# Attention and a top-1 mixture of experts on one core: six experts sorted by their token counts, with three capacities in place of one

## The chip, the cores and the metric

The kernel runs on one core of a Trainium2 chip. The metric is the device time of one execution in microseconds (us); three runs of the kernel before gave 747.33, 748.36 and 748.40 us, with a median of 748.36 us.

## The reference

Eight batches of eight heads attend causally over 576 positions with a multiplicative decay; the result, 4608 rows of 512 numbers, goes through a layer of eight experts of which each row takes one.

```
scores = q @ k.T / sqrt(64) + decay          # causal, decay from the cumulated log of f
x      = softmax(scores) @ v                 # 4608 rows x 512
logits = x @ w_gate                          # 512 x 8
e(row) = argmax(logits);  g(row) = softmax(logits)[e]
out[row] = g(row) * relu(x[row] @ w1[e]) @ w2[e]     # w1: 512 x 1024, w2: 1024 x 512
```

All inputs are float32. On the inputs that the reference draws, experts 0 to 7 receive 582, 620, 632, 571, 592, 462, 604 and 545 rows, 4608 in all.

## The kernel before

**Attention.** The first 297 us compute attention and store its rows in device memory (`x_dram`). The order of all its steps is a table of words in `attention_all` (lines 639 to 697): a word names a step, and an object that pins the program order keeps each engine to that order. After each batch, routing (`route_stages`) ranks the batch's rows within their experts; after the last batch `table_indices` (line 1049) turns the table of ranks into three arrays of 40 columns: the row to gather (`gi_fast`), the row to scatter to (`si_fast`), the gate weight (`g_fast`). Column 5e + m belongs to tile m, 128 rows, of expert e. In the table of words this is `34.ix`; `34.ef3` and `34.ef4` gather the last two tiles of expert 0, `34.en` two tiles of expert 1, `34.et3` and `34.et4` transpose the two tiles of expert 0 on TensorE.

**Experts.** Every expert has room for `CAP` = 640 rows, five tiles of 128. A slot beyond an expert's count gathers row 0, and its result is scattered to a row number out of bounds, which the scatter leaves out. Expert 0 is interleaved with the end of attention; experts 1 to 7 run one after another in `Moe.run`, each in two phases.

- *Up* (`seven`, `product`): the 640 rows are split in two halves of 320, the weight matrix in four blocks, and Strassen's method in Winograd's form makes the product out of seven block products. There are four rounds `i` of seven products, and a product is six matmuls of 128 x 128 weights on 320 columns (line 1456: two halves of the contraction, and for each float32 product three rounded products). That makes 4 x 7 x 6 = 168 matmuls for each expert. ScalarE, VectorE and GpSimd sum, apply relu and split the result into a high and a low word.
- *Down* (`down`, line 1244): for each tile of 128 rows 24 matmuls, with the rows of the hidden layer as stationary weights and 512 columns of `w2` streaming. Between them stand the transposes of the next expert's gathered rows (`turn_t`, line 1412, four for each tile). The last tile of the last expert is done in two halves of 256 columns (`down_last`, line 1267).

Weights of the next expert are loaded on SyncE's queue (SP) by `load_s` (line 1334, four DMAs of 128 KB, four times for each expert) and `load_v` (line 1380, four DMAs of 512 KB); GpSimd forms the sums of weight blocks from them (`sums_s`, lines 1340 to 1343), ScalarE and VectorE split them in two words. All steps are placed by a step number (`ups`, `dns`) and issued in that order.

**Overflow.** After the last expert `overflow` (line 1608) computes on VectorE how many rows exceed the room, loads that number into a register of every engine (line 1635), and repeats a loop (line 1639) once for each 128 rows left over. With all counts up to 640 the loop is passed over.

Of the kernel before, what the change touches and what calls it, by code (L numbers as in the profile page):

```python
# [10 lines left out]
I32 = mybir.dt.int32  # L11
# [30 lines left out]
XM = 2 * (KT // 2) * HN  # L42
XN = ("T2", "T1", "T4", "T3", "B22")
# [142 lines left out]
def attention_all(c, tc, qkT, va, vb, f, wgd, x_dram, batch_done, more_consts, extra):  # L186
# [11 lines left out]
    with ExitStack() as st:  # L198
# [413 lines left out]
        def fin_logits(b, part, pool):  # L612
# [82 lines left out]
            34.W07 34.d21 34.d02 34.d12 34.ix 34.ef3 34.d22 34.ef4 34.en 34.d13 34.et3:m 34.et4:c  # L695
# [397 lines left out]
class Moe:  # L1093
    def __init__(self, c, tc, x_dram, w1, w2, out):
        self.c, self.tc, self.nc = c, tc, tc.nc
        self.x_dram, self.w1, self.w2, self.out = x_dram, w1, w2, out
        self.w1p, self.w2p, self.xg, self.x, self.h = {}, {}, {}, {}, {}
        self.idx, self.w1raw, self.w2raw, self.py = {}, {}, {}, {}

        self.ups = 5  # L1100
# [88 lines left out]
    def index(self, e, m):  # L1189
        if e == 0 and m < NA:  # L1190
            return (*self.idx["early"], m)
        return (*self.idx["all"], e * NST + m)

# [31 lines left out]
    def rows_of_h(self, e, m):  # L1225

        if e == 0:
            h = self.h[0, 0 if m < NA else 1]
            ms = slice((m % NA) * P, (m % NA) * P + P)
            return lambda i, ft: h[i][:, ft, ms]  # L1230
        return lambda i, ft: self.h[e][i][:, ft, m * P : m * P + P]

    def down(self, e, m, part=(0, FT), pool=None):

        c, nc = self.c, self.nc
        rows = self.rows_of_h(e, m)
        _, si, g, s = self.index(e, m)
        if part[0] == 0:
            self.py[m] = psum(pool or (c.ps_v, c.ps_m)[m % 2])
        py = self.py[m]  # L1240
        for ft in range(*part):
            w = self.w2p[e, ft]
            for k, (hi_, wi) in enumerate(((0, 0), (0, 1), (1, 0))):
# [7 lines left out]
        nc.scalar.activation(y, py, AF.Copy, scale=g[:, s : s + 1])  # L1251
        self.scatter(y, si[:, s : s + 1])
# [38 lines left out]
    def steps(self):  # L1291
# [17 lines left out]
        def indices():  # L1309
# [8 lines left out]
            en=lambda: (self.fetch(1, 3), self.fetch(1, 4)),  # L1318
# [58 lines left out]
    def load_v(self, e, i):  # L1377
# [4 lines left out]
            self.w2[e, 2 * i * P : 2 * i * P + 2 * P, :].rearrange("(f p) d -> p f d", p=P),  # L1382
# [10 lines left out]
    def begin_t(self, e):  # L1393

        c = self.c
        xa = c.xap.tile([P, 2, KT, HN], F32R, name="xa", tag="xa")
        part = lambda a: a.rearrange("p (k s) -> p k s", s=HN)
# [6 lines left out]
    def turn_t(self, e, m):  # L1404
# [34 lines left out]
        z = min(max(HN - m * P, 0), P)  # L1439
        if z < P:  # L1440
            second(pt[:, :, z:], m * P + z - HN)
# [3 lines left out]
    def split_t(self, e, n, eng=None):  # L1445

        c, k = self.c, XN.index(n)
        self.round(c.words["X", k, 0], c.words["X", k, 1], c.values["X", k, 1], eng)

    def product(self, e, i, bank, part, mat, x, start):  # L1450
# [3 lines left out]
        for kt in range(KT // 2):  # L1454
            for wi, xi in ((0, 0), (1, 0), (0, 1)):
                self.nc.tensor.matmul(  # L1456
                    bank[:, 0:HN], w[:, wi, mat, kt], x[xi][:, kt, :],
# [4 lines left out]
    def seven(self, e, i, run, tasks):  # L1462
# [5 lines left out]
        a, b, g, d = (t[:, 0:HN] for t in (a, b, g, d))  # L1468
        p1, p5, u2, u3 = (self.up_.tile([P, HN], F32, name=f"u{k}") for k in range(4))
        hh, hl = self.h[e]  # L1470

        def place(h, f, n):
            return h[:, f * (FT // 2) + i, n * HN : n * HN + HN]
# [41 lines left out]
    def run(self, run, rest):  # L1515
        c, tc = self.c, self.tc
        T = lambda f, *args: lambda: f(*args)
        fetch = lambda e, m: T(self.fetch, e, m)
# [37 lines left out]
        with tc.tile_pool(name="moe_h", bufs=1) as hp, tc.tile_pool(name="moe_u", bufs=1) as up_, \  # L1556
# [3 lines left out]
            h = [t.rearrange("p (f s) -> p f s", s=CAP) for t in (c.words["hh"], hl)]  # L1560
            G = self.nc.gpsimd
            for e in range(1, E):
                self.h[e] = h
# [18 lines left out]
                if e + 1 < E:  # L1582
# [4 lines left out]
                    at(dns, (0, N(self.begin_t)), (0, N(self.turn_t, 3)), (0, fetch(e + 1, 1)),  # L1587
                       (0, N(self.split_s, 0, 0)), (1, N(self.split_s, 0, 1)),
                       (2, N(self.load_s, 2)), (2, N(self.turn_t, 4)),
                       (3, N(self.split_s, 1, 0)), (4, N(self.turn_t, 2)),  # L1590
                       (5, N(self.split_s, 1, 1)), (6, N(self.load_s, 3)),
                       (6, N(self.turn_t, 0)), (7, N(self.sums_s, 2)),
                       (8, N(self.turn_t, 1)), (9, N(self.split_s, 2, 0)),
# [9 lines left out]
                downs(e, range(NST - (e == E - 1)), dns)  # L1603
                if e == E - 1:
                    run(lambda: self.down_last(e, NST - 1))


def overflow(c, tc, x_dram, w1, w2, out):
# [5 lines left out]
    with ExitStack() as st:  # L1614
# [4 lines left out]
        V.tensor_scalar(ex, c.carry, -float(CAP), 0.0, ALU.add, ALU.max)  # L1619
# [19 lines left out]
        with tc.For_i(0, n_it) as _i:  # L1639
# [13 lines left out]
            V.tensor_scalar(rr, rr, float(P), float(CAP) - 8192.0 * E, ALU.mult, ALU.add)  # L1653
# [144 lines left out]
```

## Time and profile before

| | before |
|---|---|
| median of three runs | 748.36 us (747.33 to 748.40) |
| the profiled execution | 747.16 us |
| its span, first to last instruction | 744.9 us |
| granted TensorE clock, mean | 0.998 |
| TensorE matmul busy | 736.4 us, 99% |
| VectorE busy | 552.3 us, 74% |
| ScalarE busy | 486.1 us, 65% |
| GpSimd busy | 430.6 us, 58% |

The profiled execution took 2.3 us more than its span, and lies 1.2 us under the median of the three runs. Busy shares are means over the whole program; a stage can have another limit than the program.

### The profile page before, as it was taken

The page shows a single profiled execution, that of the slowest core. Times are in us where ns is not written, and L with a number is a line of the kernel's source. Part 1 is how long each engine was busy: PE and PEld are TensorE (multiplying, and loading weights), DVE is VectorE, ACT ScalarE, POOL GpSimd, SP SyncE. Part 2 cuts the span into 40 slices and gives each one's busy share as a digit, 9 for nine tenths or more (in the row PEclk, how much of TensorE's full clock was granted, in tenths as well). Part 3 has the DMA queues.
Part 4 walks back from the last instruction along what each step waited for, and adds up shares of the span by engine and source line. Part 5 has one row for each costly group of instructions (what it writes and reads, how often), then busy time and mean ns, then how long its engine had stood idle before and what let it go on. Part 6 is the DMA issues. An engine that isn't in the chain of part 4 may idle for free.

```text
span 744.9 us, 16310 instructions
## 1 busy us (share of the span) xinstructions
PE 736.4 (99%) x5552; PEld 612.6 (82%) x5552; DVE 552.3 (74%) x1553; ACT 486.1 (65%) x1267; POOL 430.6 (58%) x594
## 2 busy tenths in 40 slices
PE   9999999999999999999999999999999999999996
PEld 6667777777777777989998998998998988988985
DVE  8877989888889998555888488487586685784720
ACT  7899899898989996335566465464564653663621
POOL 6643656566565586634976575475475565566311
PEclk9999999999999999999999999999999999999999
DMA  7989898898989694534453523613623632523100
GB/s 221 238 211 218 217 236 224 227 233 222 243 206 248 179 258 144 174 114 127 123 170 113 181 73 114 201 57 109 205 73 100 201 97 92 180 86 126 54 29 34
DMA packets 82932, 118.41 MB, mean 159 GB/s; under 512 B 9823, under 2 KB 40543, under 8 KB 82848
## 3 DMA queue, kind: packets, MB, share of 16 engines
q1 hardware_dynamic: 75680, 97.18, 47.8%
q0 software_dynamic: 6400, 19.93, 8.1%
q8 instruction: 45, 0.74, 0.4%
q14 instruction: 39, 0.32, 0.1%
q10 hardware_dynamic: 768, 0.25, 0.1%
HBM read 98.14 MB, written 20.22 MB: 159 GB/s over the span
## 4 chain that ended last, share of the span: by engine, by line
PE 94%; POOL 2%; DVE 1%; issue 1%; DMA 0%; ACT 0%; SPq 0%; POOLq 0%; ACTq 0%
PE ps L1244 28%; PE ps L1456 19%; PE ps L548 12%; PE ps L488 12%; PE ps L418 10%; PE ps L1214 4%; PE ps L454 2%; PE pr L1456 1%; PE ps L1412 1%; PE ps L605 1%; PE ps L1267 1%; PE pr L270 1%; PE pr L1037 1%; DVE w_1w L1371 0%; POOL w1r L1341 0%
## 5 line engine op out<-in xcount | busy, mean ns | idle before, releaser
L405 ACT ACTIVATE sc<-sc,nmx 128x128 f32<-128x128 f32 (+3 forms) x256 | 142.8, 566 | 3.0 <-DVE nmx L402 2.7
L1456 PE MATMUL ps<-X_0w,w1s 128*128 128x320 f32 x504 | 112.0, 309 | 0.0
L1244 PE MATMUL ps<-w_0w,hhw 128*128 128x512 f32 x272 | 108.7, 400 | 0.0
L1244 PE MATMUL ps<-w_1w,hhw 128*128 128x512 f32 x272 | 106.9, 393 | 0.0
L1244 PE MATMUL ps<-w_0w,hl 128*128 128x512 f32 x272 | 106.3, 391 | 0.0
L402 DVE CUSTOM_DVE_ANT_0 sc<-ps,dec 128x384 f32<-128x384 f32 (+2 forms) x192 | 90.2, 507 | 10.7 <-ACT sc L405 2.2
L1276 POOL DMA_INDIRECT out<-y,si_fast x37 | 37.5, 1012 | 94.6 <-ACT y L1251 81.8
L548 PE MATMUL ps<-aT,va_t 128*64 128x256 f32 (+3 forms) x896 | 92.1, 353 | 0.0
L1456 PEld LDWEIGHTS ps<-X_0w,w1s 128*128 128x128 f32 x504 | 84.2, 188 | 0.2
L548 PEld LDWEIGHTS ps<-aT,va_t 128*64 128x64 f32 x896 | 57.4, 137 | 31.9 <-issue 6.4
L418 PE MATMUL ps<-raw 64*128 64x256 f32 (+3 forms) x512 | 81.6, 444 | 0.6 <-ACT aT L484 0.4
L1456 PE MATMUL ps<-X_1w,w1s 128*128 128x320 f32 x252 | 77.9, 309 | 0.0
L1251 ACT ACTIVATE y<-ps,g_fast 128x512 f32<-128x512 f32 x36 | 24.8, 690 | 80.7 <-PE ps L1244 59.2
L484 ACT COPY aT<-ps 128x512 f32<-128x512 f32 (+4 forms) x154 | 63.0, 452 | 12.2 <-PE ps L488 10.9
L418 PEld LDWEIGHTS ps<-raw 64*128 64x128 f32 x512 | 45.5, 186 | 26.1 <-issue 7.9
L1244 PEld LDWEIGHTS ps<-w_0w,hl 128*128 128x128 f32 x272 | 51.1, 188 | 11.3
L1498 POOL TENSOR_TENSOR u<-u,u 128x320 f32<-128x320 f32 x28 | 24.6, 880 | 61.4 <-DVE u L1496 61.3
L1244 PEld LDWEIGHTS ps<-w_0w,hhw 128*128 128x128 f32 x272 | 51.0, 188 | 10.1
L1361 DVE TENSOR_TENSOR w1s<-w1r,w1s 128x1024 fp32r<-128x1024 f32 (+1 forms) x42 | 53.2, 1279 | 8.3 <-ACT w1s L1355 8.3
L1456 PE MATMUL ps<-xa,w1s 128*128 128x320 f32 x336 | 58.7, 310 | 0.4 <-ACT u L1485 0.4
L1244 PEld LDWEIGHTS ps<-w_1w,hhw 128*128 128x128 f32 x272 | 51.1, 188 | 9.4
L1355 ACT CAST w1s<-w1r 128x1024 fp32r<-128x1024 f32 (+1 forms) x56 | 52.2, 944 | 8.7 <-POOL w1r L1341 8.0
(283 smaller groups left out, 1792.5 us busy)
## 6 DMA issues: line engine op xcount, KB each, us to landing
dec<-cd SPq DMA_DIRECT2D x30, 512.0 KB, 6.2
w1r<-in_w SPq DMA_DIRECT2D x112, 128.0 KB, 3.3
w<-in_w SPq DMA_DIRECT2D x28, 512.0 KB, 4.8
raw<-in_qkT SPq DMA_DIRECT2D x63, 160.0 KB, 6.1
raw<-in_qkT SPq DMA_DIRECT2D x64, 144.0 KB, 6.1
decj<-cd SPq DMA_DIRECT2D x30, 288.0 KB, 5.3
va_t<-in_va SPq DMA_DIRECT2D x32, 256.0 KB, 6.2
x_dram<-row SPq DMA_DIRECT2D x32, 256.0 KB, 5.5
```

The costliest lines, as they stand in the source:

```text
L402: V.tensor_tensor_reduce(dst, src, m, -0.125, init, ALU.add, ALU.min, out)
L405: nc.scalar.activation(x, x, AF.Exp, bias=nmx, scale=-1.0, accum_out=acc)
L418: note(nc.tensor.matmul(banks[j][:, o : o + w], r[:, P * t : P * t + P], r[:, QW : QW + w], start=True, stop=n > 1))
L484: nc.scalar.copy(dst, src)
L488: note(nc.tensor.transpose(out.bitcast(F32R), words, c.identr))
L548: c.last_av = note(nc.tensor.matmul(pv[j * HD : (j + 1) * HD, q0 - qa : qb - qa], l, r, start=(blk == 0), stop=(blk == nb - 1),))
L1214: c.note(nc.tensor.matmul(ph[:, 0:n], w[:, wi, fs], x[xi][:, kt, :], start=(k == 0), stop=(k == 3 * KT - 1),))
L1244: c.note(nc.tensor.matmul(py, rows(hi_, ft), w[wi], start=(ft + k == 0), stop=(ft == FT - 1 and k == 2),))
L1276: self.nc.gpsimd.indirect_dma_start(out=self.out, out_offset=bass.IndirectOffsetOnAxis(ap=rows, axis=0), in_=y, in_offset=None, bounds_che ...
L1355: self.nc.scalar.copy(t[:, 0], raw)
L1361: (eng or self.nc.vector).tensor_tensor(lo, raw, hi.bitcast(F32), ALU.subtract)
L1456: self.nc.tensor.matmul(bank[:, 0:HN], w[:, wi, mat, kt], x[xi][:, kt, :], start=start and k == 0, stop=k == 5, skip_group_check=True,)
```

## The change

The experts 0 and 1 keep room for 640 rows. The experts 2 to 7 are sorted on the chip by their counts, largest first, and take the six places 2 to 7 of the program in that order, with room for 640, 640, 640, 576, 576 and 512 rows (`CAPS`). With 576 rows the halves have 288 columns, with 512 they have 256; a place of 576 has a last tile of 64 rows, the place of 512 has four tiles.

`sort` (`34.so`, seven VectorE operations) makes a key from each count, compares all pairs, and gives the expert's number for each place as an integer; `sort_table` (`34.st`, ten operations) puts the three index arrays into the order of the places by a masked sum. `expert` loads the expert's number from SBUF into a register of SP, once for each place, and `load_s` and `load_v` use that register in the addresses of the weights. `overflow` compares each count with its own capacity.

The diff, cut:

```diff
+NF = 2
+SORTED = E - NF
+CAPS = [CAP] * (E - 3) + [576, 576, 512]
...
-            34.W07 34.d21 34.d02 34.d12 34.ix 34.ef3 34.d22 34.ef4 34.en 34.d13 34.et3:m 34.et4:c
+            34.W07 34.d21 34.so 34.d02 34.d12 34.ix 34.ef3 34.d22 34.ef4 34.en 34.st 34.d13 34.et3:m 34.et4:c
...
+        if e >= NF:
+            return (*self.idx["sorted"], (e - NF) * NST + m)
...
+    def sort(self):
...
+        V.scalar_tensor_tensor(keys, c.carry[:, NF:E], float(E), c.iota128[:, NF:E],
+                               ALU.mult, ALU.add)
...
+        V.tensor_tensor(sel, keys.unsqueeze(1).to_broadcast([P, n, n]),
+                        keys.unsqueeze(2).to_broadcast([P, n, n]), ALU.is_gt)
...
+        V.tensor_reduce(rank, sel, AX.X, ALU.add)
...
+        V.tensor_copy(c.ids, ids)
...
+    def sort_table(self):
...
+        for nm, x in (("gi", gi), ("si", si), ("g", g)):
...
+            t = rp.tile([P, n, NST, n], F32, name="so_w")
...
+            V.tensor_reduce(y.rearrange("p (s m) -> p s m", m=NST), t, AX.X, ALU.add)
...
+    def expert(self, e):
...
+            v = self.nc.values_load(self.c.ids[0:1, e - NF : e - NF + 1],
+                                    engines=[mybir.EngineType.SP], min_val=NF, max_val=E - 1)
...
-        py = self.py[m]
+        n = min(P, CAPS[e] - m * P)
+        py = self.py[m][0:n]
...
+        w = self.expert(e)
         block = lambda f, d: self.w1[
-            e, d * 2 * P : d * 2 * P + 2 * P, (f * (FT // 2) + i) * P :][:, 0:P].rearrange(
+            w, d * 2 * P : d * 2 * P + 2 * P, (f * (FT // 2) + i) * P :][:, 0:P].rearrange(
...
-            self.w2[e, 2 * i * P : 2 * i * P + 2 * P, :].rearrange("(f p) d -> p f d", p=P),
+            self.w2[self.expert(e), 2 * i * P : 2 * i * P + 2 * P, :].rearrange(
...
+        n = CAPS[e] // 2
+        a, b, g, d = (t[:, 0:n] for t in (a, b, g, d))
...
-        fetch = lambda e, m: T(self.fetch, e, m)
+        fetch = lambda e, m: T(lambda: m * P < CAPS[e] and self.fetch(e, m))
+        turn_t = lambda e, m: T(lambda: m * P < CAPS[e] and self.turn_t(e, m))
...
+                tiles = -(-CAPS[e] // P)
+                downs(e, range(tiles - (e == E - 1)), dns)
...
-        V.tensor_scalar(ex, c.carry, -float(CAP), 0.0, ALU.add, ALU.max)
+        caps = op.tile([P, E], F32, name="ov_caps")
+        V.memset(caps, float(CAP))
...
+        for s in range(SORTED):
+            V.tensor_scalar(capm[:, :, s], c.so_sel[:, s], float(CAPS[NF + s]), None, ALU.mult)
+        V.tensor_reduce(caps[:, NF:], capm, AX.X, ALU.add)
+        V.tensor_tensor(ex, c.carry, caps, ALU.subtract)
+        V.tensor_scalar(ex, ex, 0.0, None, ALU.max)
```

Three places of the program show how instructions move.

VectorE at the end of routing, before; `tab` is the table of ranks, `xb` the low word of expert 0's last two tiles:

```order
L1041 TENSOR_TENSOR tab<-tab,pr 128x240
L1055 SCALAR_TENSOR_TENSOR ti_fast<-tab 128x40
L1057 CAST gi_fast<-ti_fast 128x40
L1059 TENSOR_SCALAR tu_fast<-tab 128x40
L1060 TENSOR_TENSOR ti_fast<-ti_fast,tu_fast 128x40
L1062 CAST si_fast<-ti_fast 128x40
L1064 TENSOR_TENSOR g_fast<-tab 128x40
L1065 TENSOR_TENSOR g_fast<-g_fast,tab 128x40
L1185 TENSOR_TENSOR xb<-ps,xb 128x4x128 x2
```

The same place with the change, as far as the index that the gathers wait for:

```order
L1044 TENSOR_TENSOR tab<-tab,pr 128x240
L1205 SCALAR_TENSOR_TENSOR so_key<-rk,iota_336 128x6
L1208 TENSOR_TENSOR so_sel<-so_key 128x36
L1211 TENSOR_REDUCE so_rank<-so_sel 128x6
L1213 TENSOR_TENSOR so_sel<-so_rank,iota_336 128x36
L1217 TENSOR_TENSOR so_t<-so_sel,iota_336 128x36
L1219 TENSOR_REDUCE so_ids<-so_t 128x6
L1221 CAST so_idi<-so_ids 128x6
L1058 SCALAR_TENSOR_TENSOR ti_fast<-tab 128x40
L1060 CAST gi_fast<-ti_fast 128x40
L1062 TENSOR_SCALAR tu_fast<-tab 128x40
```

The seven operations of `sort` stand between the table and `gi_fast`, `tu_fast`; the ten of `sort_table` follow `g_fast` and stand before `xb`.

SP, where the loads of expert 1's `w2` end and those for place 2 begin, before:

```order
L1334 DMA w1r<-in_w 128x2x128 x4
L1380 DMA w_0_1_94<-in_w 128x2x512 x2
L1380 DMA w_1_1_100<-in_w 128x2x512 x2
L1334 DMA w1r<-in_w 128x2x128 x16
L1380 DMA w_0_1_94<-in_w 128x2x512 x2
```

and with the change:

```order
L1447 DMA w_0_1_94<-in_w 128x2x512 x2
L1447 DMA w_1_1_100<-in_w 128x2x512 x2
L1254 TENSOR_LOAD so_idi
L1254 ISA x2
L1401 ISA
L1401 DMA w1r<-in_w 128x2x128
```

A load of a register with two instructions behind it comes once for each place, and from there on each DMA has an instruction of its own ahead of it.

VectorE at the end of the program, before:

```order
L1619 TENSOR_SCALAR ov_ex<-rk 128x8
L1626 MEMSET ov_one 128x8
L1634 MEMSET ov_cnt 128x1
L1622 TENSOR_TENSOR ov_cm<-ov_ex,iotaP 128x288
L1624 TENSOR_REDUCE ov_ex<-ov_cm 128x8
L1628 SCALAR_TENSOR_TENSOR ov_inc<-ov_one,ov_ex 128x8
L1630 TENSOR_TENSOR ov_exc<-ov_inc,ov_ex 128x8
L1632 CAST ov_tot<-ov_inc 1x1
```

and with the change:

```order
L1695 MEMSET ov_caps 128x8
L1698 TENSOR_SCALAR ov_capm<-so_sel 128x6 x6
L1708 MEMSET ov_one 128x8
L1716 MEMSET ov_cnt 128x1
L1699 TENSOR_REDUCE ov_caps<-ov_capm 128x6
L1700 TENSOR_TENSOR ov_ex<-rk,ov_caps 128x8
L1701 TENSOR_SCALAR ov_ex<-ov_ex 128x8
L1704 TENSOR_TENSOR ov_cm<-ov_ex,iotaP 128x288
L1706 TENSOR_REDUCE ov_ex<-ov_cm 128x8
L1710 SCALAR_TENSOR_TENSOR ov_inc<-ov_one,ov_ex 128x8
L1712 TENSOR_TENSOR ov_exc<-ov_inc,ov_ex 128x8
L1714 CAST ov_tot<-ov_inc 1x1
```

Nine operations more stand ahead of the integer that every engine loads.

## Rows read from the trace of the kernel before

**Rows 1.** The page: the span and its instructions
```profile
span 744.9 us, 16310 instructions
```

**Rows 2.** Stretches: length, then busy PE, PEld, DVE, ACT, POOL, clock, DMA share
```profile
632.66:657.30 24.64, 24.64 (x170) 24.64 (x169) 18.39 (x32) 15.23 (x29) 14.64 (x13) 1.00 0.47 144
686.68:711.31 24.63, 24.63 (x169) 24.63 (x169) 18.35 (x33) 15.23 (x29) 7.26 (x6) 1.00 0.21 77
```

**Rows 3.** Chain that ended last, experts 6 and 7: start, us, what
```profile
642.34 11.44 PE ps L1456 x78
...
711.31 21.97 PE ps L1244 x96
733.28 5.45 PE ps L1267 x48
```

**Rows 4.** The same chain while expert 0 ends
```profile
332.60 0.64 PE ps L1179 x8
...
336.09 5.75 PE ps L1214 x48
```

**Rows 5.** Groups by line and form, and the chain: matmuls with 64-column weights
```profile
L548 PE MATMUL ps<-aT,va_t 128*64 128x256 f32 x384 | 47.8, 384 | 0.0
...
L548 PE MATMUL ps<-aT,va_t 128*64 128x192 f32 x256 | 31.7, 326 | 0.0
...
L548 PE MATMUL ps<-aT,va_t 128*64 128x320 f32 x128 | 23.5, 445 | 0.0
...
L548 PE MATMUL ps<-aT,vb 68*64 68x64 f32 x128 | 9.1, 220 | 0.0
L548 PE MATMUL ps<-aT,va_t 128*64 128x64 f32 x128 | 9.1, 220 | 0.0
...
127.58 2.87 PE ps L548 x32
```

**Rows 6.** Timeline of VectorE and GpSimd at the end of routing, and the gathers' landing
```profile
326.12 0.20 DVE L1055 SCALAR_TENSOR_TENSOR ti_fast<-tab 128x40 f32<-128x40 f32 x1
326.36 0.18 DVE L1057 CAST gi_fast<-ti_fast 128x40 uint32<-128x40 f32 x1
326.45 0.18 DVE L1059 TENSOR_SCALAR tu_fast<-tab 128x40 f32<-128x40 f32 x1
...
326.82 1.09 POOL L1165 DMA_INDIRECT xg<-x_dram,gi_fast  x1 [2.89 <-DVE tu_fast L1059]
328.21 0.95 POOL L1165 DMA_INDIRECT xg<-x_dram,gi_fast  x1 [0.30 <-issue]
...
DMA to landing us min/median/max: 3.4/3.4/3.4
```

**Rows 7.** Lines L1635 and L1334 on SP: ns min/median/max
```profile
L1635 SPq TENSOR_LOAD <-ov_tot x1: 469/469/469, 740.5 to 740.5; - x1
...
L1635 SPq FUSED_REGOPS  x1: 186/186/186, 741.0 to 741.0; - x1
...
L1334 SPq DMA_DIRECT2D w1r<-in_w x112: 367/465/1121, 320.9 to 669.7; - x112
```

**Rows 8.** Expert 7's weight loads: SP, landing, and the sums on GpSimd
```profile
663.38 6.84 SPq L1334 DMA_DIRECT2D w1r<-in_w  x8
...
DMA to landing us min/median/max: 2.1/2.7/3.6
...
671.83 0.77 POOL L1340 TENSOR_TENSOR w1r<-w1r 128x256 f32<-128x256 f32 x1
...
677.77 1.34 POOL L1340 TENSOR_TENSOR w1r<-w1r 128x256 f32<-128x256 f32 x1
```

**Rows 9.** The end: VectorE, the last scatter, and what SP waited for
```profile
738.76 0.17 DVE L1619 TENSOR_SCALAR ov_ex<-rk 128x8 f32<-128x8 f32 x1 [25.09 <-PE ps L1267]
...
739.51 0.98 POOL L1276 DMA_INDIRECT out<-y,si_fast  x1 [4.19 <-ACT y L1271]
740.24 0.13 DVE L1632 CAST ov_tot<-ov_inc 1x1 int32<-1x1 f32 x1
...
SPq L1639 <- DMA out<-y,si_fast: 0.6, 1, 0.6
```

**Rows 10.** DMA queues, whole span: the gathers and scatters (packets, MB, share)
```profile
q0 software_dynamic: 6400, 19.93, 8.1%
```

More of the change, by code (lines that the diff above doesn't have):

```diff
@@ new lines, in sort_table @@
+    def sort_table(self):
+        c, nc = self.c, self.nc
+        V, rp, n = nc.vector, c.rp, SORTED
+        gi, si, g = self.idx["all"]
+        mine = []
+        for nm, x in (("gi", gi), ("si", si), ("g", g)):
+            if nm != "g":
+                x_ = rp.tile([P, n * NST], F32, name=f"so_{nm}f")
+                V.tensor_copy(x_, x[:, NF * NST :])
+            else:
+                x_ = x[:, NF * NST :]
+            t = rp.tile([P, n, NST, n], F32, name="so_w")
+            V.tensor_tensor(
+                t, c.so_sel.unsqueeze(2).to_broadcast([P, n, NST, n]),
+                x_.rearrange("p (e m) -> p m e", m=NST).unsqueeze(1).to_broadcast(
+                    [P, n, NST, n]), ALU.mult)
+            y = rp.tile([P, n * NST], F32, name=f"so_{nm}y")
+            V.tensor_reduce(y.rearrange("p (s m) -> p s m", m=NST), t, AX.X, ALU.add)
+            if nm != "g":
+                u = rp.tile([P, n * NST], U32, name=f"so_{nm}")
+                V.tensor_copy(u, y)
+                y = u
+            mine.append(y)
+        self.idx["sorted"] = tuple(mine)
@@ L1194, in begin_h @@
+    def expert(self, e):
+        if e < NF:
+            return e
+        if e not in self.ids:
+            v = self.nc.values_load(self.c.ids[0:1, e - NF : e - NF + 1],
+                                    engines=[mybir.EngineType.SP], min_val=NF, max_val=E - 1)
+            self.ids[e] = v
+        return self.ids[e]
     def begin_h(self, e, chunk):
@@ L1250, in down @@
         y = c.yp.tile([P, D], F32, name="y")
[L1251 to L1252 removed]
+        nc.scalar.activation(y[0:n], py, AF.Copy, scale=g[0:n, s : s + 1])
+        self.scatter(y[0:n], si[0:n, s : s + 1])
     def down_last(self, e, m):
@@ L1447, in split_t @@
         c, k = self.c, XN.index(n)
-        self.round(c.words["X", k, 0], c.words["X", k, 1], c.values["X", k, 1], eng)
+        part = lambda a: a.rearrange("p (k s) -> p k s", s=HN)[:, :, 0 : CAPS[e] // 2]
+        self.round(*(part(a) for a in (c.words["X", k, 0], c.words["X", k, 1],
+                                       c.values["X", k, 1])), eng)
     def product(self, e, i, bank, part, mat, x, start):
@@ L1467, in seven, with place @@
         a, b, g, d = [psum(p) for p in pools] + [c.ps_r] * (i % 2)
-        a, b, g, d = (t[:, 0:HN] for t in (a, b, g, d))
-        p1, p5, u2, u3 = (self.up_.tile([P, HN], F32, name=f"u{k}") for k in range(4))
+        n = CAPS[e] // 2
+        a, b, g, d = (t[:, 0:n] for t in (a, b, g, d))
+        p1, p5, u2, u3 = (self.up_.tile([P, HN], F32, name=f"u{k}")[:, 0:n] for k in range(4))
         hh, hl = self.h[e]
-        def place(h, f, n):
-            return h[:, f * (FT // 2) + i, n * HN : n * HN + HN]
+        def place(h, f, k):
+            return h[:, f * (FT // 2) + i, k * n : k * n + n]
         def relu(src, *at):
@@ L1602, in run @@
                 dns.setdefault(0, [])[:0] = self.ends
-                downs(e, range(NST - (e == E - 1)), dns)
+                tiles = -(-CAPS[e] // P)
+                downs(e, range(tiles - (e == E - 1)), dns)
                 if e == E - 1:
-                    run(lambda: self.down_last(e, NST - 1))
+                    run(lambda: self.down_last(e, tiles - 1))
 def overflow(c, tc, x_dram, w1, w2, out):
```

51 lines of the change are left out of this document (36 added, 15 removed).

## The prediction

> **What bounds the kernel now.** The page comes first: a span of 744.9 us [rows 1], in which the profiled execution took 747.16 us. The page's shares by engine are means, so I read the expert part in stretches that begin where the up phase and the down phase of an expert begin. In the up phases of experts 6 and 7 TensorE is busy for the whole stretch, 24.64 and 24.63 us, at a granted clock of 1.00, that is 2.4 GHz, while VectorE is busy 18.4 us, ScalarE 15.2 us and GpSimd 14.6 or 7.3 us [rows 2]. The reader is to see that no engine but TensorE fills its stretch. The chain of work that ended last says the same: through the last two experts it runs from TensorE to TensorE [rows 3]. So from the first expert to the last matmul a matmul less is time less, as long as the other engines keep up, and a wait of TensorE is time more.
>
> **What a column costs.** The change takes columns away from matmuls, so their spacing is needed at three widths. 78 matmuls of 320 columns take 11.44 us, 146.7 ns each [rows 3]; 48 matmuls of 256 columns, the same kind of product in expert 0, take 5.75 us, 119.8 ns each [rows 4]. That is 26.9 ns for 64 columns, 0.42 ns for a column. The trace has none of these products at 288 columns; halfway between the two gives 133.2 ns. The nearest other row is that of the last tile, 48 matmuls of 256 columns in 5.45 us, 113.5 ns each [rows 3], where the stationary operand is another. I take 119.8 ns because the product is the same, and keep 113.5 ns for the range.
>
> **Up phases.** Places 5 and 6, with 576 rows, keep 168 matmuls each: 2 x 168 x 13.45 ns = 4.5 us less. Place 7, with 512 rows: 168 x 26.9 ns = 4.5 us less.
>
> **Down phases.** Place 7 has four tiles instead of five, so 24 matmuls of 512 columns go. 96 of them take 21.97 us [rows 3], 228.9 ns each: 24 x 228.9 ns = 5.5 us less. Its fifth gather and four transposes go too; eight such transposes take 0.64 us [rows 4], so 0.3 us less. The fifth tile of a place of 576 rows has 64 rows, but I give nothing for that: its rows are the stationary operand, and 512 columns still stream. The trace shows a bound: in attention the weights have 64 columns, the 1024 matmuls of five forms carry 204,800 columns, and 32 of them (6400 columns) take 2.87 us, 0.448 ns for a column [rows 5], against 228.9 / 512 = 0.447 ns with 128. Half a weight tile is not faster.
>
> All that TensorE loses: 4.5 + 4.5 + 5.5 + 0.3 = 14.8 us.
>
> **The sort, ahead of the gathers.** Seven VectorE operations go in ahead of the index array. Nearest are the index operations themselves: one that waits for its predecessor starts 0.24 us after it, one that doesn't 0.09 us after it [rows 6]. Six of the seven wait: about 1.5 us, between 0.7 and 1.8 us. The gathers of expert 0's last two tiles wait on GpSimd for exactly these index operations and start at 326.82 and 328.21 us; they land 3.4 us later [rows 6], the second at 331.6 us. Its transposes are the last four of the eight that begin at 332.60 us [rows 4], so they need it at 332.9 us, or some 0.3 us earlier if their weights are loaded ahead. A slack of 1.0 to 1.3 us meets a delay of 1.5 us: I take 0.4 us of wait on TensorE, between 0 and 0.8 us. Behind this wait stand expert 0's last down matmuls and everything after them, so it is paid in full. The two gathers for expert 1 and the two scatters behind them on GpSimd move by the same 1.5 us and have no transposes so near. The ten operations of the table follow the arrays the first gathers use; they cost about 3 us of a VectorE that has nothing in its queue before the low words of expert 0's last rows, which wait for those transposes. I cost them at nothing; without that cover it would be those 3 us.
>
> **Weights by register.** For each place SP loads a register, 0.47 us, with an operation on registers of 0.19 us behind it, and each DMA gets one instruction, which I price like that operation, 0.19 us [rows 7]. SP is a queue of its own and no computation stands behind it. What matters is the slack of a load. For expert 7, eight DMAs are issued in 6.84 us from 663.38 us, and landing takes at most 3.6 us; GpSimd sums the first four from 671.83 us and the last four from 677.77 us [rows 8]. Four issues at 0.47 us [rows 7] and the landing put the first four at 668.9 us and the last four at 670.2 + 3.6 = 673.8 us. The slack is 2.9 and 4.0 us, the added time 0.8 and 1.5 us: nothing is paid. As a bound for an issue by register I take the longest issue in the trace, 1.12 us against a median of 0.47 us [rows 7]; below, nothing. The two tables of gathers and scatters are read at other addresses only, which moves nothing.
>
> **The other engines in shorter phases.** The shortest up phase becomes 24.63 - 4.5 = 20.1 us. Even if no VectorE operation got shorter, its 18.35 us [rows 2] would fit, and most of them do shrink with the columns. I cost this at nothing too; the rival below prices it.
>
> **The end.** The overflow test can't begin before TensorE is done. From its first operation at 738.76 us to the integer at 740.37 us it takes 1.6 us, beside the last scatter, and SP then still waits 0.6 us for that scatter [rows 9]. The change puts nine operations more ahead of it: seven of them wait for none of the others, 0.1 us each, two more wait, 0.2 us each [rows 6], 1.1 us together. 0.6 us of that lies under the scatter: 0.5 us to pay, between 0 and 1.1 us.
>
> **Sum.** -14.8 + 0.4 + 0.5 = -13.9 us. Against its own time the profiled execution would take 747.2 - 13.9 = 733.3 us, with a span of 731.0 us. It lies 1.2 us under the median of the three runs; against the median the forecast is **734.5 us**.
>
> **The rivals.** (1) *Weights come late.* If an issue by register costs the full 1.12 us, eight issues last 8 x 0.66 = 5.3 us longer against a slack of 4.0 us. Each of six places then waits 1.3 us: 734.5 + 8 = 742 us. For it: the loads are the one thing that no row shows by register. Against it: the register operation that the trace does show takes 0.19 us. Chance 8%.
>
> (2) *The up phases don't shrink as TensorE does*, because each product's sums on VectorE, ScalarE and GpSimd free the PSUM banks for the next. If half of their 9 us stays, 739 us. For it: VectorE already fills three quarters of the up phase. Against: it isn't full even in 20.1 us. Chance 7%.
>
> (3) *The spacing is set by the weight load, not by the columns.* Each of these matmuls brings its own 128 x 128 weights, and PEld is busy throughout the up phase [rows 2]. Then the up phases keep their length and only the tile goes: 748.4 - 5.8 + 0.9 = 743.5 us. Against it stand the 119.8 ns at 256 columns with weights of the same size [rows 4]. Chance 2%. The Trainium skill, TensorE: Matmul & The Clock Gate, section Back-to-back issue gap, speaks for a weaker form of it: for streams of weight loads with matmuls it gives about 81 ns at 128 columns and 131 ns at 512, which is 0.13 ns for a column. By that, as an estimate, the up phases would give 2.8 us instead of 9.0 us. This trace doesn't agree, with 228.9 ns at 512 columns.
>
> (4) *An expert doesn't fit, and the kernel becomes slower.* The counts of the six are 632, 604, 592, 571, 545 and 462: room enough, the tightest by five rows. Should one place overflow by a single row, the loop runs once: twelve indirect loads in sequence on GpSimd at about 1.0 us of issue each and 3.4 us of landing [rows 6], then unsplit float32 matmuls, a gather and a scatter, each after the other: at least 20 us, and it decides as soon as it runs at all. 734.5 + 20 = 755 us or more. For it: a margin of five rows. Against it: the counts are fixed by the inputs, and the 40 gathers and 40 scatters moved 19.93 MB [rows 10]; 40 gathers of 128 rows of 2 KB are 10.49 MB, which leaves 9.44 MB, or 4608 rows: every row went through a regular tile. Chance 4%.
>
> **How the numbers follow.** The forecast has 79%. Its own bounds: with 113.5 ns at 256 columns the up phases give 11.1 us instead of 9.0 us, and without the two waits another 0.9 us goes, so 731.5 us; with both waits at their upper end 735.5 us, and half a microsecond either way for the run. The low end stands there. To leave no more than 2 in 10 out, the high end reaches into the second rival, 739.5 us. What a measurement of this kernel can tell from no change is about 0.2%, 1.5 us. The forecast and the first three rivals are all faster by more than that, 96%; I take off 3% for a mixture of them, or a wait that no row shows: faster 0.93, the same 0.02, slower 0.05.
>
> **What would show it.** Right: in the groups by line, products of 288 and 256 columns, spaced 133 and 120 ns in the chain; up phases of 22.4, 22.4 and 20.1 us; a last down phase of 96 matmuls instead of 120; TensorE still busy throughout. A wait of TensorE for a gather near 333 us shows the sort's price, a test of some 2.7 us at the end that of the overflow. Wrong: waits of TensorE for split weights or for PSUM in every place (rivals 1 and 2), a spacing that stays at 147 ns (rival 3), or instructions of the overflow loop (rival 4).

## The result, and the profile after

The changed kernel takes **738.5 us** (median of four runs, 737.92 to 738.88); the kernel before took 748.33 us in the four runs beside it (747.33 to 748.40). The ratio is 0.9871, with a 95% interval of 0.9854 to 0.9888: faster, by 9.8 us or 1.3%. The forecast was 734.5 us, 13.9 us less, with a range of 731.5 to 739.5 us. So the direction held, the time lies inside the range, and 4 us of the gain are missing.

The profiled execution took 738.52 us. Its page begins like this; in [rows 1] the span is 744.9 us:

```profile
span 736.7 us, 16523 instructions
```

By spans the gain is 8.2 us; the profiled execution of before lay 1.2 us under its median, that of after on it. The rest goes by spans, since both traces can be laid side by side.

The same view by stretches as [rows 2], now for the up phases of experts 2 (room 640), 6 (576) and 7 (512); columns: length, busy PE, PEld, DVE, ACT, POOL, clock, DMA share, GB/s.

```profile
417.29:441.93 24.64, 24.64 (x170) 24.64 (x169) 18.24 (x32) 15.21 (x29) 14.59 (x13) 1.00 0.48 154
632.60:655.39 22.79, 22.54 (x169) 22.31 (x168) 16.98 (x30) 14.46 (x29) 12.20 (x12) 1.00 0.46 151
684.70:706.30 21.60, 20.73 (x169) 20.14 (x168) 16.25 (x30) 13.87 (x29) 6.74 (x6) 1.00 0.23 85
```

TensorE fills the first stretch, as before. It no longer fills the other two, at the same clock: 0.25 and 0.87 us of them are idle. The waits of TensorE from 350 us to the end (us in total, how many, the longest):

```profile
PE ps L1528 <- ACT u L1558: 1.6, 5, 0.7
PE ps L1333 <- ACT y L1317: 0.8, 1, 0.8
PE ps L1528 <- ACT u L1564: 0.2, 1, 0.2
```

The same view of the kernel before has the first of these waits too, under other line numbers, and a wait for a gather:

```profile
PE ps L1456 <- ACT u L1485: 0.4, 2, 0.2
PE ps L1412 <- DMA xg<-x_dram,gi_fast: 0.2, 1, 0.2
```

In both kernels two of the waits for ScalarE's copy, 0.4 us, stand in expert 1's up phase, which has room 640. The other three of after, 0.2 us of line 1564 and the 0.8 us before the last tile are new, and all lie at the experts with smaller rooms.

To find what these don't say, I took from the two traces the start of the first matmul of each phase (up: line 1528; down: lines 1310 and 1333) and set the lengths beside the terms of the sum, in us:

| term | forecast | before | after | difference |
|---|---|---|---|---|
| start of expert 1's up phase (gather wait) | +0.4 | 361.06 | 361.29 | +0.2 |
| up phases 1 to 4 | 0 | 26.05, then 24.63 | 26.22, then 24.63 | +0.2 |
| up phases 5 and 6 | -4.5 | 24.63 | 22.80 | -3.7 |
| up phase 7 | -4.5 | 24.63 | 21.60 | -3.0 |
| down phases 1 to 6, sum | -0.3 | 176.24 | 177.70 | +1.5 |
| down phase 7, to its last matmul | -5.5 | 27.30 | 23.42 | -3.9 |
| from there to the span's end | +0.5 | 6.45 | 6.96 | +0.5 |
| sum | -13.9 | | | -8.2 |

Three places miss their forecast: the up phases by 2.3 us, the last down phase by 1.6 us, and the other down phases by 1.8 us, which were to gain 0.3 us. Those of experts 1 to 5 became 0.2 to 0.5 us longer each, experts with room 640 among them, whose products the change doesn't touch; only that of expert 6, where four transposes go, is 0.1 us shorter.

**What came as forecast.** The spacing of the products: in the chain of waits of after, where no wait stands between them,

```profile
632.76 7.96 PE ps L1528 x60
...
684.86 6.41 PE ps L1528 x54
```

that is 132.7 ns at 288 columns and 118.7 ns at 256, forecast 133.2 and 119.8 ns. With the 146.7 ns at 320 columns [rows 3] the three lie on a line of 0.44 ns for a column, where the forecast had 0.42 ns. The sustained figures of the Trainium skill, TensorE: Matmul & The Clock Gate, section Back-to-back issue gap, by which the prediction estimated 0.13 ns for a column, don't hold for these products.

The loads by register address: three kinds of instructions of line 1401 (before: 1334, [rows 7]) in ns, min/median/max:

```profile
L1401 SPq DMA_DIRECT2D w1r<-in_w x112: 367/373/1851, 321.1 to 666.7; - x112
L1401 SPq FUSED_REGOPS  x96: 46/46/56, 374.0 to 666.5; - x96
L1401 SPq MOVE w1r<-in_w x96: 29/29/38, 374.2 to 666.6; - x96
```

An address costs 46 + 29 = 75 ns on SP, where 190 ns were reckoned. No wait of TensorE comes from a weight load: rival 1 is out. The end, on VectorE:

```profile
730.05 0.16 DVE L1698 TENSOR_SCALAR ov_capm<-so_sel 128x6 f32<-128x6 f32 x1 [20.81 <-issue]
...
732.51 0.13 DVE L1714 CAST ov_tot<-ov_inc 1x1 int32<-1x1 f32 x1
```

The test takes 2.6 us where [rows 9] had 1.6 us, and the end got 0.5 us longer, the size that was summed; the part on the prediction says why this agreement shows little. The overflow loop didn't run.

### The profile page after: what moved, and what is told of

Same layout as the page of the kernel before. It is cut to its first block, busy times and chain, and to the rows that moved or that the text cites. A ratio compares the mean times of both kernels' runs of the same rounds, so it can differ in the third digit from the quotient of the medians.

```text
span 736.7 us, 16523 instructions
## 1 busy us (share of the span) xinstructions
PE 725.0 (98%) x5524; PEld 596.7 (81%) x5524; DVE 550.5 (75%) x1573; ACT 480.6 (65%) x1263; POOL 425.7 (58%) x592
## 4 chain that ended last, share of the span: by engine, by line
PE 84%; DVE 6%; issue 4%; POOL 2%; ACT 1%; DMA 1%; SPq 0%; POOLq 0%; DVEq 0%; ACTq 0%
PE ps L1310 26%; PE ps L1528 15%; PE ps L551 12%; PE ps L491 12%; PE ps L421 9%; PE ps L1279 4%; PE ps L457 2%; DVE w_1w L1438 2%; PE ps L1481 1%; DVE hl L1552 1%; PE ps L608 1%; POOL u L1571 1%; PE pr L1528 1%; DMA dec<-cd 1%; PE pr L1040 1%
## 5 line engine op out<-in xcount | busy, mean ns | idle before, releaser
L1528 PE MATMUL ps<-X_0w,w1s 128*128 128x320 f32 (+2 forms) x504 | 106.7, 301 | 0.2 <-ACT u L1564 0.2
L1310 PE MATMUL ps<-w_0w,hhw 128*128 128x512 f32 (+1 forms) x264 | 106.3, 403 | 0.0
L1310 PE MATMUL ps<-w_0w,hl 128*128 128x512 f32 (+1 forms) x264 | 104.2, 395 | 0.0
L1310 PE MATMUL ps<-w_1w,hhw 128*128 128x512 f32 (+1 forms) x264 | 103.9, 394 | 0.0
L1342 POOL DMA_INDIRECT out<-y,so_si x29 | 29.9, 1032 | 79.4 <-ACT y L1317 61.6
L1528 PE MATMUL ps<-X_1w,w1s 128*128 128x320 f32 (+2 forms) x252 | 75.7, 300 | 0.0
L1310 PEld LDWEIGHTS ps<-w_0w,hl 128*128 128x128 f32 (+1 forms) x264 | 48.6, 184 | 12.7
L1528 PE MATMUL ps<-xa,w1s 128*128 128x320 f32 (+2 forms) x336 | 56.3, 303 | 1.7 <-ACT u L1558 1.6
L1310 PEld LDWEIGHTS ps<-w_1w,hhw 128*128 128x128 f32 (+1 forms) x264 | 48.9, 185 | 10.9
L1310 PEld LDWEIGHTS ps<-w_0w,hhw 128*128 128x128 f32 (+1 forms) x264 | 48.7, 184 | 10.8
```

The source lines that it names most:

```text
L1310: c.note(nc.tensor.matmul(py, rows(hi_, ft), w[wi], start=(ft + k == 0), stop=(ft == FT - 1 and k == 2),))
L1342: self.nc.gpsimd.indirect_dma_start(out=self.out, out_offset=bass.IndirectOffsetOnAxis(ap=rows, axis=0), in_=y, in_offset=None, bounds_che ...
L1528: self.nc.tensor.matmul(bank, w[:, wi, mat, kt], x[xi][:, kt, :], start=start and k == 0, stop=k == 5, skip_group_check=True,)
```

## The experiments

**The kernel before, once more.** No edit. It says how far two traces of one program agree.

> The kernel before, once more, for its matmul spacing. Theory A (the spacing of the down matmuls belongs to the execution or its clock phase): the down phases of experts 2 to 6 come out anywhere between 29.38 us, as in the first profile, and 29.8 us, as in the profile of the change. Theory B (the change's layout or its loads by register slow them): all of them are 29.38 us within 0.03 us again, and 747.2 us within 0.3 us in all.

Its profiled execution took 746.94 us, span 744.8 us. Down phases 2 to 6 and up phases 2 to 7 agree with the first trace to 0.01 us; the first up phase began at 360.87 instead of 361.06 us. So a steady 0.25 us in a down phase is a difference, and 0.2 us at the first up phase is none.

**Sorting without smaller rooms.** Sort, registers and the new test stay; every room is 640.

```diff
-CAPS = [CAP] * (E - 3) + [576, 576, 512]
+CAPS = [CAP] * E
```

> The sort, the registers and the longer overflow test alone: all places keep 640 rows. My theory (the sort costs 0.4 us of wait for a gather, the test at the end 0.5 us, loads by register nothing): 0.9 us above the kernel before, 749.2 us, up phases of 24.64 us. Rival 1 (loads by register come late): TensorE waits for split weights in six places, 742 + 15 = about 756 us. Theory B of the spacing: down phases of 29.6 to 29.8 us, so about 751 us; theory A: the spacing tells nothing of the change.

751.89 us against 747.09 us, ratio 1.0056 [1.0036, 1.0077]: 4.2 us lost by the ratio and by the spans, 4.8 us by the medians. The up phases stay at 24.63 us, but the down phases are 29.63 or 29.78 us throughout instead of 29.38 us, and the last is 27.71 instead of 27.30 us. So the longer down phases come with the sort, the registers and the test, not with the rooms. TensorE's last matmul starts at 740.82 us (before 738.45); behind it lie 8.2 us instead of 6.45 us, the last of them a wait of SP for TensorE's queue at the very end.

**Smaller rooms without sorting.** The order of the experts for these inputs is written into the kernel; sort, registers and the new test go.

```diff
+ORDER = (0, 1, 2, 6, 4, 3, 7, 5)
...
-            return (*self.idx["sorted"], (e - NF) * NST + m)
+            return (*self.idx["all"], ORDER[e] * NST + m)
```

> The smaller rooms alone: the order of the experts (0, 1, 2, 6, 4, 3, 7, 5) is written into the program, no sort, no table, no registers, the old overflow test. My theory: 0.9 us under the change, 737.6 us, with the same waits in the up phases of the last three places (22.8, 22.8 and 21.4 us) and the same wait of about 1 us before the last tile. Theory B of the spacing: the down phases are back at 29.38 us, and the time is another 2 us lower, 735.6 us. If registers cost more than the profile shows: lower than 735 us.

735.74 us, ratio 0.9835 [0.9807, 0.9864], span 734.0 us. The up phases 5 to 7 are 22.78, 22.79 and 21.64 us, as in the changed kernel: their missing 2.3 us belong to the rooms. The down phases of experts 2 to 5 are back at 29.38 or 29.39 us, and the last one is 23.12 instead of 23.42 us: what they had lost comes with the sort. The program's end, with the old test, is 6.82 us here.

**ScalarE's copy first.** In the short up phases TensorE waits for ScalarE's copy of its first product (line 1558). The chain of waits of after shows why, at the end of expert 6's up phase:

```profile
647.96 2.43 DVE w_1w L1438 x2
650.39 0.37 DVE hl L1552
650.75 0.37 DVE u L1569
...
651.29 0.81 POOL u L1571
652.11 0.02 issue
652.13 0.02 ACT hhw L1549
652.15 0.33 issue
652.48 0.39 ACT u L1558
652.87 0.04 issue
652.91 2.65 PE ps L1528 x18
```

Two splits of down weights keep VectorE for 2.43 us; the sums `u3` and `p5` of one round stand behind them, ScalarE's relu behind those, and the copy that the next round's TensorE needs is behind the relu in ScalarE's order. The experiment moves the copy ahead of it.

```diff
             if s == 0:
-                self.ends.pop(0)()
                 A.copy(p1, a)
+                self.ends.pop(0)()
                 self.ends.pop(0)()
```

> The change with one ScalarE copy moved: the copy of product a out of its bank is issued ahead of the two relus of the round before, which wait for GpSimd. My theory (TensorE waits for this copy because it stands behind those relus in ScalarE's queue): the waits of TensorE for the copy, 1.6 us in five waits and some more in the chain, go, the up phases of the last three places become 22.4, 22.4 and 20.2 us, 2.1 us less, 736.4 us. Rival (VectorE is too full in the short phases): TensorE waits for another product's sum, and less than 1 us is gained.

737.22 us, ratio 0.9862 [0.9832, 0.9891], not to be told from the changed kernel. In its trace the waits moved rather than went:

```profile
PE ps L1528 <- ACT u L1564: 1.5, 5, 0.4
PE ps L1333 <- ACT y L1317: 0.8, 1, 0.8
PE ps L1481 <- DMA xg<-x_dram,gi_fast: 0.2, 1, 0.2
```

Line 1564 is the copy of the third product into `p5`, whose one buffer VectorE still reads. The up phases are 22.61, 22.91 and 21.31 us, and the first one 25.75 us instead of 26.22 us. So the order on ScalarE is not the only link; the single buffer of `p5` looks like another, which the experiment with two buffers tries.

**Down phases and addresses.** What does the sort leave behind for loops that run 100 us later? Its tiles take 2080 bytes of a pool, and every tile behind them moves by as much. In the compiled programs the hidden layer's low word `hl` starts at byte 188032 in the kernel before, a multiple of 128, and at 190112 after, a multiple of 32 only. So 32 idle bytes in the *kernel before* should make its down phases longer, and 32 more in the changed one shorter.

```diff
+    V.memset(rp.tile([P, 8], F32, name="pad"), 0.0)
```

> The kernel before with 32 bytes more in the pool of the routing's constants (one tile that nothing reads), so that all pools above it, and with them the low words hl, begin at an odd multiple of 32 bytes, as in the change, where the sort's tiles add 2080 bytes. Alignment theory: the down phases become 29.6 to 29.8 us and the last one 27.7 us, some 2.3 us in all, 749.4 us. Rival (the loads by register, or the place of the instructions in memory, set the spacing): 29.38 us and 747.1 us as before.

> The change with the same 32 bytes more: 2112 bytes, a multiple of 64. Alignment theory: down phases of 29.38 us again, 29.1 us for the one ahead of the last place, the last one shorter by 0.4 us, 2 us less than the change, 735.5 to 736.5 us by the clock of this chip. Rival: no difference. If 64 bytes are not enough and 128 are asked: no difference either, and the next kernel that is shifted by 2304 bytes shows it.

The kernel before with 32 idle bytes takes 749.53 us against 747.46 us, ratio 1.0028 [1.0018, 1.0039]. Its down phases are 29.63 and 29.78 us, the last one 27.71 us: those of the experiment with equal rooms, with no sort in the program. The changed kernel with the pad takes 736.67 us, ratio 0.9860 [0.9844, 0.9877], span 734.5 us, with down phases of 29.46 to 29.52 us. That repairs two thirds; `hl` is now at 190144, a multiple of 64. One row of the chain of waits shows the size, the 66 matmuls that end expert 6's down phase, first in the kernel before, then in after:

```profile
671.49 15.19 PE ps L1244 x66
...
669.48 15.38 PE ps L1310 x66
```

**The bank of the last tile.** After the last whole tile TensorE stands idle before the two half tiles. TensorE in the timeline of after:

```profile
722.86 0.40 PE L1310 MATMUL ps<-w_0w,hl 128*128 128x512 f32 x1
724.09 0.39 PE L1333 MATMUL ps<-w_0w,hhw 128*128 128x256 f32 x1 [0.83 <-ACT y L1317]
```

Whole tiles end in alternate PSUM pools, and `down_last` always begins in `ps_v`. With five tiles the last whole one, number 3, ended in the other pool; with four it is number 2, and it ends in `ps_v`, which ScalarE must empty first.

```diff
-        for o, pool in ((0, c.ps_v), (n, c.ps_m)):
+        first, then = (c.ps_v, c.ps_m) if m % 2 == 0 else (c.ps_m, c.ps_v)
+        for o, pool in ((0, first), (n, then)):
```

> The change with the two PSUM banks of the last tile taken in the other order when its number is odd. My theory (the last tile, now number 3 and no longer 4, begins in the bank that tile 2 has only just filled, and waits for ScalarE to empty it): the wait of 0.8 us before the last tile goes and the last down phase is 1.0 us shorter, 22.4 us. Rival (the wait belongs to the end of the stage and moves to the second half of the tile): no gain.

738.25 us, ratio 0.9879 [0.9862, 0.9895]: by the medians nothing. In the trace the wait is gone, the last down phase is 22.33 instead of 23.42 us and the span 735.7 instead of 736.7 us. One microsecond is no more than the interval of these medians, so the trace decides on the wait, and the medians alone would not have found it.

**Splits earlier.** If VectorE's two neighbouring splits are the trouble, let the first of them stand earlier, and with it the one before.

```diff
-                   (8, S(self.split_s, 3, 0)), (9, S(self.split_v, 0)),
+                   (8, S(self.split_s, 3, 0)), (9 if e == 1 else 6, S(self.split_v, 0)),
...
-                   (15, S(self.split_v, 1)), (16, S(self.split_v, 2)),
+                   (15 if e == 1 else 10, S(self.split_v, 1)), (16, S(self.split_v, 2)),
```

> The change with the splits of two of four w2 parts placed earlier in the up phase, at steps 6 and 10 instead of 9 and 15 (not for expert 1), so that no round has two of them on VectorE. My theory (VectorE's queue, with 2.4 us of these splits in round 2, makes the sums late that ScalarE's copy and TensorE wait for): the up phases of places 5 and 6 become 22.4 us instead of 22.8 us, that of place 7 at most 21.0 us instead of 21.6 us; together 1 to 2 us. Rival (the chain through GpSimd and ScalarE is too long by itself): no change in the up phases.

743.95 us, ratio 0.9950 [0.9933, 0.9966]: some 5 us worse than the changed kernel, which I had not expected. Even the up phases with room 640 grow, to 25.1 us; the short ones are 23.80, 23.81 and 23.85 us. VectorE in expert 6's up phase says why:

```profile
640.20 0.46 DVE L1570 TENSOR_TENSOR ps<-u,ps 128x288 f32<-128x288 f32 x1
641.02 1.23 DVE L1438 TENSOR_TENSOR w_1w<-w,w_0w 128x1024 fp32r<-128x1024 f32 x1 [0.35 <-ACT w_0w L1437]
642.16 0.46 DVE L1576 TENSOR_TENSOR ps<-ps,u 128x288 f32<-128x288 f32 x1
```

At step 6 the split stands between the last sums of a round (1570 and 1576), waits for ScalarE's half of it, and holds the second sum back by 2 us; in after 1576 follows 1570 within 0.4 us:

```profile
638.08 0.46 DVE L1570 TENSOR_TENSOR ps<-u,ps 128x288 f32<-128x288 f32 x1
638.45 0.46 DVE L1576 TENSOR_TENSOR ps<-ps,u 128x288 f32<-128x288 f32 x1
```

A place in the queue that looks free is not one when the work waited for comes right behind it.

**Two buffers, or GpSimd.** Two more ways at the up phases, both on the padded kernel. One has the copy first and two buffers each for `p1` and `p5`; the other gives the second of the two neighbouring splits to GpSimd.

```diff
-        p1, p5, u2, u3 = (self.up_.tile([P, HN], F32, name=f"u{k}")[:, 0:n] for k in range(4))
+        p1, p5, u2, u3 = (self.up_.tile([P, HN], F32, name=f"u{k}", bufs=2 if k < 2 else 1)[:, 0:n] for k in range(4))
```

> The changed kernel with the 32-byte pad (as aligned), the copy of a's bank ahead of the ends (as copy_first), and two buffers each for p1 and p5. Theory of the queue (TensorE waits in the short up phases because ScalarE's copies wait for the one p1 and the one p5 that VectorE and GpSimd still read, behind VectorE's weight splits): the waits for L1558 and L1564 go, the up phases of the experts in rooms five to seven fall from 22.8, 22.8 and 21.5 us to 22.4, 22.4 and 20.1, and with the 0.5 us that the first up phase won in copy_first the time is about 734 us against aligned's 736.7. Theory of the load (VectorE and ScalarE have too much work for a phase of 20 to 22 us, whatever the buffers): the wait turns up at another line, the up phases stay within 0.2 us each and the time is 736 or more.

```diff
-                   (15, S(self.split_v, 1)), (16, S(self.split_v, 2)),
+                   (15, S(self.split_v, 1)), (16, S(self.split_v, 2, G)),
```

> The changed kernel with the pad, and the second of two neighbouring splits of down weights on VectorE (the rest of part 2) given to GpSimd, in every expert. Theory of the queue: of the 2.3 us that two splits keep VectorE, 1.2 go, and the waits that stand behind them: each short up phase 0.2 to 0.4 us shorter, about 735.8 us against aligned's 736.7; the waits behind the single splits of parts 0, 1 and 3 stay. Theory that the two engines slow each other or that the sum on GpSimd (L1571) now waits behind a split of 2.4 us: no change or up to 1 us more, 736.5 to 737.7.

With two buffers: 736.06 us, ratio 0.9856 [0.9837, 0.9875], by medians not to be told from the padded kernel; its span is 733.3 against 734.5 us. The up phases are 22.47, 22.48 and 21.00 us against 22.81, 22.82 and 21.48 us: 576 rows reach their forecast of 22.4 us, 512 rows stay 0.9 us above theirs. So the theory of the queue holds for two of three. In the third TensorE now waits for a sum of VectorE, and why VectorE is late there wasn't tried:

```profile
PE ps L1529 <- DVE u L1562: 0.7, 1, 0.7
```

With GpSimd: 738.22 us, ratio 0.9879 [0.9864, 0.9894], and up phases of 23.06, 23.10 and 21.83 us, longer than with the pad alone. GpSimd in expert 6's up phase:

```profile
648.31 2.41 POOL L1439 TENSOR_TENSOR w_1w<-w,w_0w 128x1024 fp32r<-128x1024 f32 x1 [0.69 <-ACT w_0w L1438]
650.67 0.80 POOL L1572 TENSOR_TENSOR u<-u,u 128x288 f32<-128x288 f32 x1
```

The split takes 2.41 us there, 1.23 us on VectorE, and the sum of `p5`, for which ScalarE waits, now starts where it ends. Here an engine that is half idle was no help, because it owns one link of the chain.

**All that helped.** Pad, copy first, two buffers, the bank by the tile's number, the sort behind the first gathers of expert 1, and the rooms for the test reckoned with the sort:

```diff
-            34.W07 34.d21 34.so 34.d02 34.d12 34.ix 34.ef3 34.d22 34.ef4 34.en 34.st 34.d13 34.et3:m 34.et4:c
+            34.W07 34.d21 34.d02 34.d12 34.ix 34.ef3 34.d22 34.ef4 34.en 34.so 34.st 34.d13 34.et3:m 34.et4:c
...
-        caps = op.tile([P, E], F32, name="ov_caps")
+        caps = c.caps
```

> All that helped or should: pad, copy ahead, double p1 and p5, banks of the last tile by its number, the sort after the first fetches of expert 1, and the rooms for the overflow reckoned in the sort. If the parts add: double's time less 1.0 (bank wait), 0.4 (gather wait) and 0.3 (overflow chain), some 732.3 us if double comes to 734. If the bank wait's gain of 1 us is not in the times without a profile, as bank's median suggests (738.25 against 738.5), 733.3.

**733.64 us** (733.08 to 734.77, five runs) against 747.07 us, ratio 0.9820 [0.9806, 0.9833]: faster than both kernels, the intervals of the two ratios lie apart. Its span is 731.2 us; the forecast for the change alone had been 731.0 us. The reckoned rooms lie in the sort's pool too, 192 bytes, so `hl` starts at 190336, again a multiple of 128, and the down phases are 29.38 us again. Its chain through the last two experts, the form of [rows 3]:

```profile
638.50 10.27 PE ps L1536 x78
...
666.06 15.18 PE ps L1317 x66
681.24 5.77 PE ps L1536 x48
...
702.47 16.49 PE ps L1317 x72
718.96 5.67 PE ps L1341 x48
```

Through expert 6 nothing stands between one TensorE row and the next but 0.04 us of issue; in expert 7's up phase, 21.2 us long, a stretch on VectorE is left between 687 and 701 us.

**Equal rooms, aligned.** The experiment with equal rooms and 96 idle bytes, so that `hl` starts at a multiple of 128 (190208).

```diff
+    V.memset(rp.tile([P, 24], F32, name="pad"), 0.0)
```

> The sort, the registers and the sorted overflow test with room for 640 rows everywhere, as in same_room, and 96 bytes of padding, by which the tile hl starts at a multiple of 128 bytes as in the kernel before. Theory of the address (what the sort adds to the loops over the experts is only the place of its neighbours): the down phases of experts 2 to 6 fall from 29.6 and 29.8 us to 29.4, the last from 27.7 to 27.3, in all some 2.4 us less than same_room; what stays is the gather's wait and the longer end, and the time is 0.9 to 2.2 us above before's (748 to 749.3 against 747.1). Theory that the sort's own work or the loads by register address cost it: the down phases stay as in same_room and the time is 751 or more.

750.10 us against 748.03 us, ratio 1.0024 [1.0015, 1.0033], where it had been 1.0056. Every down phase from the second on is 29.37 us, the last 27.31 us, and TensorE's last matmul starts at 738.07 us, no later than in the kernel before. So for the loops over the experts the sort and the registers cost nothing but their tiles' place. What is left lies behind the last matmul: 8.5 us instead of 6.45 us. VectorE's test ends 1.0 us later, and SP's last wait for TensorE's queue is longer:

```profile
SPq L1881 <- PEq L1881: 2.8, 2, 2.0
```

It was 1.7 us in the kernel before and 1.3 us in after. Why the two kernels with a sort and equal rooms have it, and no other, stays open: in all the others at most 7.3 us lie behind the last matmul.

## Why the prediction was right, and where it was wrong

**Right.** The bound: TensorE sets the pace, and columns taken from it come back at 0.44 ns each where nothing waits; [rows 3, 4] gave 0.42 ns from two widths. The register loads: 75 ns an address, and no wait. Rivals 1, 3 and 4 are out by rows.

**Luck.** By the spans the three misses come to 5.7 us, all in one direction, against a forecast of 13.9 us. The high end of the range was set by rival 2, which came at half its price, 2.3 us; nearly all the rest comes from two terms that the sum doesn't have, the addresses and the bank. That the time still lies inside the range is in part luck.

So is the end, +0.5 us forecast and measured. The test did become 1.0 us longer. But the experiment without a sort, whose test is the old one, has 6.82 us behind the last matmul, and the best version, whose test is 0.2 us longer than the old one, has 6.83 us, against 6.96 us with the change and 6.45 us before. In both, SP's wait for the last scatter ends 4.2 us after the last matmul's start, in the kernel before 3.7 us after it. With equal rooms and the longer test it ends after 4.3 us. So either alone makes SP late, and most of the 0.5 us is there without the longer test; why the scatter is late with the smaller rooms is open.

**The gather wait** was forecast at 0.4 us, "paid in full". It is there in after:

```profile
329.65 3.59 DMA xg<-x_dram,gi_fast
333.24 0.04 issue
333.29 0.54 PE ps L1183 x4
```

The view of waits gives 0.3 us. But it isn't paid in full. The first down matmul behind these transposes starts 0.6 us later than before, the first up phase 0.2 us, which is about what two traces of the kernel before differ by. In the padded kernel the same wait is 0.6 us, and the first up phase begins at 360.78 us, earlier than before's 361.06 us. Between the two points TensorE stands still twice more in the kernel before, ahead of transposes of expert 1's rows: 0.1 us at 345.5 us, and 0.2 us for a gather at 350.9 us (its line stands under the result). In after only the second is left, with 0.1 us, and in the padded kernel neither: a part of the delay takes the place of waits that were there anyway. The step that failed is "behind this wait stand expert 0's last down matmuls and everything after them, so it is paid in full": I followed TensorE's order and didn't ask where it would wait again further on.

**Up phases** ("I cost this at nothing"): 2.3 us short. This is rival 2, at half the price I gave it. Read as idle time, the waits are 0.25, 0.25 and 0.87 us, while the phases miss their forecast by 0.4, 0.4 and 1.5 us: an idle stretch costs more than it lasts. At expert 6's wait the matmuls start 0.54 and 0.24 us apart instead of 0.13 us, 0.5 us lost for 0.25 us of idle. VectorE's busy time did fit, as I wrote; but a sum of busy times says nothing of a chain that goes round VectorE, GpSimd and ScalarE once a round. Its links don't shrink with the columns where they are splits of weights (two take 2.43 us at 288 columns and 2.36 us at 256), and it closes through single buffers. Two buffers and another order won 0.3 us in each phase of 576 rows and 0.5 us in that of 512.

**The last down phase** ("24 matmuls of 512 columns go"): the price of 228.9 ns each was right, the best version's 27.30 - 22.03 = 5.3 us shows it. What I left out is that one tile less changes the parity of the last one: 1.1 us, shown by the experiment on the bank. I counted the matmuls of a tile and didn't ask which bank the next one finds. Another 0.3 us is the address again (23.42 us against 23.12 us without the sort). Some 0.2 us is another spacing of the half tiles, 118.1 ns instead of 113.5 ns in [rows 3], which stands in all versions with room 512, however aligned; its cause is open.

**The other down phases**: +1.8 us against the forecast, from a term that isn't in the sum at all. Shown by 32 idle bytes, which do the same to the kernel before, and by the versions in which it goes. I asked of each new tile what its operations cost, and not what its size does to the tiles behind it.

The expert 1 up phase's 0.2 us is open; it is there in the experiment without a sort and in the kernel before with 32 idle bytes as well (26.23 and 26.20 us).

## What to carry to other kernels

When work is taken from the engine that bounds a loop, ask two things of every neighbour: does the chain that goes round the other engines once per round close in the shorter time, and does a count that changed its parity still meet a free buffer? A tile added anywhere ahead moves the tiles behind it: where loops that a change doesn't touch become slower by a steady part, compare start addresses before anything else, and try a pad that brings them back to multiples of 128 bytes. And a gain of one microsecond, which medians can't show, can be read off the lengths of phases: those of the later experts repeated here to 0.01 us from one trace of a program to the next.

## What the runs showed of the hardware that I had not expected

The spacing of matmuls depends on where tiles start in SBUF. Mean length of down phases 2 to 4, 120 matmuls of 512 columns and 20 transposes each, beside the start of `hl` in the compiled program:

| start of `hl` | kernels | down phase |
|---|---|---|
| multiple of 128 | before, smaller rooms without sorting, best, equal rooms aligned | 29.37 to 29.38 us |
| of 64, not 128 | changed with the pad | 29.49 us |
| of 32, not 64 | changed, before with the pad, equal rooms | 29.63 and 29.78 us, in turn |

All tiles behind the pad move with `hl`, so it marks the offset and need not be the cause. Indeed the products that read only `hhw`, which doesn't move, slow down as well: in down phases 2 and 3 of the kernel before, `w_0w` by `hhw` takes 229.5 ns from start to start, with 32 idle bytes 234.7 and 231.6 ns. Which operand or which other engine's access it is, was not tried. At room for 640 rows it comes to 0.3 us per expert.
